# A written order for layer norm and SwiGLU forward, turned loads instead of TensorE turns, and stores on GpSimd's queue

## The chip, the cores and the metric

The kernel runs on one core of one Trainium2 chip. The metric is the time of one execution on the device in microseconds (us), as the median of several executions. A core has five engines with instruction streams of their own: TensorE (PE, with its weight loads PEld), VectorE (DVE), ScalarE (ACT), GpSimd (POOL) and SyncE (SP). A transfer (DMA) is issued by one of them and stands in the queue of that engine; 16 DMA engines move the data. A "turned load" is one DMA that writes the transpose of its source: rows become columns on the way. Turning can also be done on TensorE, as a matmul with the identity, whose result then has to be copied out of PSUM.

## The reference

The block is `x + s * silu(SwiGLU(LN(x)))`, where s comes from attention with a recurrent memory (64 segments of 32 tokens, 8 memory rows, 32 heads of 128). The kernel returns the output and the gradients of x, the initial memory, four attention weights and three SwiGLU weights. S is 2048 tokens, D is 640, F is 1728; everything is bf16.

```python
def _layernorm(x, axis=-1, eps=1e-05):
    m = jnp.mean(x, axis=axis, keepdims=True)
    v = jnp.var(x, axis=axis, keepdims=True)
    return (x - m) / jnp.sqrt(v + eps)

def _B_ref(x, w1, w3, w2):                      # SwiGLU
    gate = jnp.einsum('bsd,df->bsf', x, w1)
    up = jnp.einsum('bsd,df->bsf', x, w3)
    h = _silu(gate) * up
    return jnp.einsum('bsf,fd->bsd', h, w2)

xn = _layernorm(x, axis=-1)
s = _A_ref(xn, A_mem0, A_Wq, A_Wk, A_Wv, A_Wo, A_seg_len)   # recurrent attention, not shown
g = _silu(_B_ref(xn, B_w1, B_w3, B_w2))
out = x + s * g
# reference(): jax.vjp of this, applied to grad_out; returns out and nine gradients
```

## The kernel before

The program goes through these stages, one after the other: layer norm; SwiGLU forward; projections of the first tokens for the attention ("b0"); the forward chain over the memory; its output; the backward chain; the attention's weight gradients; the gradient of Wo; the gradient of w2; the SwiGLU backward with the layer norm backward; the gradients of w1 and w3. The change touches the beginning and the end, and in the middle only the loads of turned activations.

Layer norm, per tile of 128 tokens (16 tiles), and then the SwiGLU forward, per block of 512 tokens. `XN` and `XNT` are the normed activations in DRAM, straight and turned; `SLT` and `DUT` are two factors that the backward needs; `HB` is the hidden activation:

```python
            xn = io.tile([P, D], BF16, name="xn_t", tag="xn_t")
            nc.vector.tensor_scalar(xn[:], xt[:], rs, nmr[:], op0=ALU.mult, op1=ALU.add)
            k.dma(k.XN[tt * P:(tt + 1) * P, :], xn[:])
            # 5 TensorE transposes into pt, a copy, and the store of XNT
...
        nc.gpsimd.dma_start(Wv[:], k.A_Wv.rearrange("(dc p) h e -> p dc (h e)", p=P))
        k.x_rows(k.HRO, k.XN, nc.gpsimd)
        for blk in range(NBLK):
            if blk == 1:
                nc.gpsimd.dma_start(Wk_[:], k.A_Wk.rearrange("(dc p) h e -> p dc (h e)", p=P))
            b0 = blk * BLK
            xnT = io.tile([P, DC, BLK], BF16, name="xnT_b", tag="xnT_b")
            nc.scalar.dma_start(xnT[:], k.XNT[:, b0:b0 + BLK].rearrange("(dc p) t -> p dc t", p=P))
            hBT = io.tile([P, FC, BLK], BF16, name="hBT", tag="hBT")
            for fc in range(FC):                       # 14 chunks of hidden columns, the last has 64
                # 5 matmuls into pg (gate), 5 into pu (up), 512 columns each
                nc.scalar.activation(sig[:fsz], pg[:fsz], ACT.Sigmoid)
                nc.vector.tensor_tensor(sl[:fsz], pg[:fsz], sig[:fsz], ALU.mult)
                nc.scalar.copy(ut[:fsz], pu[:fsz])
                nc.vector.tensor_tensor(hBT[:fsz, fc, :], sl[:fsz], ut[:fsz], ALU.mult)
                nc.vector.scalar_tensor_tensor(ds[:fsz], sig[:fsz], 1.0, sl[:fsz], op0=ALU.subtract, op1=ALU.mult)
                nc.vector.tensor_tensor(ds[:fsz], sig[:fsz], ds[:fsz], ALU.subtract)
                nc.vector.tensor_tensor(ds[:fsz], ds[:fsz], ut[:fsz], ALU.mult)
                nc.sync.dma_start(k.SLT[fc * P:fc * P + fsz, b0:b0 + BLK], sl[:fsz])
                nc.sync.dma_start(k.DUT[fc * P:fc * P + fsz, b0:b0 + BLK], ds[:fsz])
            for ti in range(BLK // P):                 # second half, per 128 tokens
                # 28 matmuls of 320 columns (hBT with w2s) into pz; gb, dz, gs on VectorE and their stores on SP
                # 5 TensorE transposes of gs (store of GST), 14 of hBT, copies, store of HB
```

The first attention projection begins with the turned activations:

```python
        xs = io.tile([P, DC, k.NB0], BF16, name="b0x")
        nc.sync.dma_start(xs[:], k.XNT[:, 0:k.NB0].rearrange("(dc p) t -> p dc t", p=P))
```

The end of the kernel: gradient of w2 (`w2a`), SwiGLU backward in blocks of 256 tokens (`pghb`, `pgxb`, the turns `ptt5`), gradients of w1 and w3 (`wa`):

```python
                    for tt in range(NT):
                        pt = psA.tile([P, DC, P], BF16, name="gzp", tag="gzp")
                        for dc in range(DC):
                            nc.tensor.transpose(pt[:, dc, :], gz[:, tt, dc * P:(dc + 1) * P], k.ident[:])
                        k.copy(gzT[:, :, tt * P:(tt + 1) * P], pt[:], eng='vs'[tt % 2])
                    # w2a: 28 accumulators, 16 matmuls of 320 columns each, from hb and gz; stores of out9 on SP
...
                    for b0 in range(0, S, BLK):        # 8 blocks
                        for f0 in range(0, FC, 2):
                            # loads of two chunks of SLT and DUT (sl5, du5) on ScalarE's queue
                            for c in range(2):
                                # 5 matmuls of 256 columns (w2T with gzT) into pg ("pghb", two buffers)
                                nc.vector.tensor_tensor(ggT[0:fsz, fc, :], pg[0:fsz, :], du[0:fsz, c, :], ALU.mult)
                                nc.vector.tensor_tensor(guT[0:fsz, fc, :], pg[0:fsz, :], sl[0:fsz, c, :], ALU.mult)
                        for ti in range(BLK // P):
                            # 56 matmuls of 320 columns into pgx ("pgxb", one buffer); every fourteenth has 64 rows
                            for i, (gT, dst) in enumerate(((ggT, ggtok[:, tt, :]), (guT, gut[:]))):
                                pt = psC.tile([P, 2 * 1024], BF16, name="ptt5", tag="ptt5", bufs=2)
                                for fc in range(FC):
                                    fsz = fszs[fc]
                                    nc.tensor.transpose(pt[:, fc * P:fc * P + fsz], gT[0:fsz, fc, tcol], k.ident[0:fsz, 0:fsz])
                                nc.vector.tensor_copy(dst[:, 0:704], pt[:, 0:704])
                                nc.scalar.copy(dst[:, 704:F], pt[:, 704:F])
                            nc.sync.dma_start(GU[rows, :], gut[:])
                            # layer norm backward: gxn and six more operations; out1 stored on SP
...
                gutok = up.tile([P, NT, F], BF16, name="gutok_all")
                # 8 loads of GU; then 320 matmuls of 432 columns on ggtok, 320 on gutok ("wa")
```

Of the kernel before, what the change touches and what calls it, by code (L numbers as in the profile page):

```python
# [9 lines left out]
BF16 = mybir.dt.bfloat16  # L10
# [30 lines left out]
class K:  # L41
# [55 lines left out]
    def setup_consts(self):  # L97
# [9 lines left out]
        self.mean_all = const.tile([P, self.NT], F32, name="mean_all")  # L107
# [44 lines left out]
    def setup_dram(self):  # L152
# [7 lines left out]
        self.XNT = mk("XNT", (D, S))  # L160
        self.SLT = mk("SLT", (F, S))
        self.DUT = mk("DUT", (F, S))
        self.HB = mk("HB", (S, F))
# [3 lines left out]
        self.GST = mk("GST", (D, S))  # L167
# [200 lines left out]
def phase3_Afwd(k, W4, Wv, Wk_):  # L368
# [5 lines left out]
    with tc.tile_pool(name="b0", bufs=1) as io, tc.tile_pool(name="b0s", bufs=3) as stp, \  # L374
            tc.tile_pool(name="b0p", bufs=4, space=bass.MemoryType.PSUM) as ps:
        xs = io.tile([P, DC, k.NB0], BF16, name="b0x")
        nc.sync.dma_start(xs[:], k.XNT[:, 0:k.NB0].rearrange("(dc p) t -> p dc t", p=P))
# [21 lines left out]
    with tc.tile_pool(name="ast", bufs=1) as st, tc.tile_pool(name="achain", bufs=1) as ch, \  # L399
# [22 lines left out]
        def ride_ld(t):  # L422
            x0 = k.NB0 + 24 * t
            b, sub = t // 4, t % 4
            if sub == 0 and x0 < S:
                w = min(96, S - x0)
                rt = ch.tile([P, DC, 96], BF16, name="ride", tag="ride")
                nc.sync.dma_start(rt[:, :, 0:w], k.XNT[:, x0:x0 + w].rearrange("(dc p) s -> p dc s", p=P))
                rides[b] = (rt, w)
# [339 lines left out]
def gx_ld(k, xs, x0, eng):  # L769
    w = min(P, k.S - x0)  # L770
    eng.dma_start(xs[:, :, 0:w], k.GST[:, x0:x0 + w].rearrange("(dc p) t -> p dc t", p=P))
# [13 lines left out]
def phase3b_out(k, Wo, W0, W4):  # L785
# [12 lines left out]
    with tc.tile_pool(name="oio", bufs=1) as io, tc.tile_pool(name="oac", bufs=1, space=bass.MemoryType.PSUM) as pa, \  # L798
# [60 lines left out]
        def gox_ld(x0):  # L859
            xs = io.tile([P, DC, P], BF16, name="g0x", tag="g0x", bufs=2)  # L860
            gx_ld(k, xs, x0, nc.scalar)
            st["gx", x0] = xs
# [61 lines left out]
def phase4_Abwd(k, out2, WoT, WvT, WkT, WqT, later):  # L924
# [3 lines left out]
    with tc.tile_pool(name="gst", bufs=1) as st, tc.tile_pool(name="gchain", bufs=1) as ch, \  # L928
# [25 lines left out]
        def ride_ld(t):  # L954
# [3 lines left out]
            if sub == 3:  # L958
                rt = ch.tile([P, DC, 96], BF16, name="gride", tag="gride")
                nc.sync.dma_start(rt[:], k.GST[:, 96 * b:96 * b + 96].rearrange("(dc p) s -> p dc s", p=P))  # L960
# [278 lines left out]
        def gox(x0, cg, b):  # L1239
            if cg == 0 and b == 0:  # L1240
                uu["gx"] = ch.tile([P, DC, P], BF16, name="gx0", tag="xp", bufs=1)
                gx_ld(k, uu["gx"], x0, nc.gpsimd)
# [252 lines left out]
def phase6b_gWo(k, gow, orr0, out6, gz, late):  # L1495
# [4 lines left out]
    with tc.tile_pool(name="o6", bufs=1) as hp, tc.tile_pool(name="o6i", bufs=2) as io, \  # L1500
# [21 lines left out]
        def rows_ld(q):  # L1522
            orrs[q] = io.tile([P, NW, 512], BF16, name="orr", tag="orr")
            for a in range(2):
                rows = slice(h * P * a, h * P * (a + 1))
                nc.sync.dma_start(orrs[q][:, h * a:h * a + h, :],
                                  k.OR[rows, 512 * q:512 * q + 512].rearrange("(t p) c -> p t c", p=P))
        rows_ld(1)
        for qd in range(8):
            orr = orrs[qd]  # L1530
            for jp in range(2):
# [4 lines left out]
                if qd > 1 and late:  # L1536
                    out_, in_ = late.pop(0)
                    if in_ is k.w2:
                        turned_load(k, out_, in_)
                    else:  # L1540
                        nc.scalar.dma_start(out_, in_)
# [8 lines left out]
                for j in range(2):  # L1550
# [4 lines left out]
                    nc.sync.dma_start(out6f[hh * P:(hh + 1) * P, :], ot[:])  # L1555
# [5 lines left out]
def phase1_ln(k: K):  # L1561
    nc, tc = k.nc, k.tc
    D, DC, NT = k.D, k.DC, k.NT
    with tc.tile_pool(name="ln_io", bufs=3) as io, tc.tile_pool(name="ln_sm", bufs=4) as sm, \
            tc.tile_pool(name="ln_ps", bufs=2, space=bass.MemoryType.PSUM) as ps:
        half = D // 2
        assert half <= nc.vector.BN_STATS_FMAX
        for tt in range(NT):
            xt = io.tile([P, D], BF16, name="xt", tag="xt")
            k.dma(xt[:], k.A_x[tt * P:(tt + 1) * P, :])  # L1570
            stats = sm.tile([P, 2, nc.vector.BN_STATS_DIM], F32, name="stats", tag="stats")
            xv = xt[:].rearrange("p (a b) -> p a b", a=2)
            nc.vector.bn_stats(stats[:, 0, :], xv[:, 0, :])
            nc.vector.bn_stats(stats[:, 1, :], xv[:, 1, :])
            mv = sm.tile([P, nc.vector.BN_AGGR_DIM], F32, name="mv", tag="mv")
            nc.vector.bn_aggr(mv[:], stats[:])
            rs = k.rstd_all[:, tt:tt + 1]
            nc.scalar.activation(rs, mv[:, 1:2], ACT.Sqrt, bias=k.eps_t[:], scale=1.0)
            nc.vector.reciprocal(rs, rs)
            nc.vector.tensor_copy(k.mean_all[:, tt:tt + 1], mv[:, 0:1])  # L1580
            nmr = sm.tile([P, 1], F32, name="nmr", tag="nmr")
            nc.vector.tensor_tensor(nmr[:], mv[:, 0:1], rs, ALU.mult)
            nc.vector.tensor_scalar(nmr[:], nmr[:], -1.0, None, op0=ALU.mult)
            xn = io.tile([P, D], BF16, name="xn_t", tag="xn_t")
            nc.vector.tensor_scalar(xn[:], xt[:], rs, nmr[:], op0=ALU.mult, op1=ALU.add)
            k.dma(k.XN[tt * P:(tt + 1) * P, :], xn[:])
            pt = ps.tile([P, DC, P], BF16, name="lnT", tag="lnT")
            for dc in range(DC):
                nc.tensor.transpose(pt[:, dc, :], xn[:, dc * P:(dc + 1) * P], k.ident[:])
            xnT = io.tile([P, DC, P], BF16, name="xnT_t", tag="xnT_t")  # L1590
            k.copy(xnT[:], pt[:])
            k.dma(k.XNT[:, tt * P:(tt + 1) * P].rearrange("(dc p) t -> p dc t", p=P), xnT[:])

def phase2_Bfwd(k: K, Wv, Wk_):
    nc, tc = k.nc, k.tc
    D, DC, S, F, FC = k.D, k.DC, k.S, k.F, k.FC
    BLK = 512
    NBLK = S // BLK  # L1600
    fszs = [min(P, F - fc * P) for fc in range(FC)]
    with tc.tile_pool(name="bw", bufs=1) as wp, tc.tile_pool(name="bio", bufs=2) as io, \
            tc.tile_pool(name="bwork", bufs=2) as wk, \
            tc.tile_pool(name="bps", bufs=2, space=bass.MemoryType.PSUM) as ps, \
            tc.tile_pool(name="bps1", bufs=1, space=bass.MemoryType.PSUM) as ps1:
        w1s = wp.tile([P, DC, F], BF16, name="w1s")
        k.dma(w1s[:], k.w1.rearrange("(dc p) f -> p dc f", p=P))
        w3s = wp.tile([P, DC, F], BF16, name="w3s")
        k.dma(w3s[:], k.w3.rearrange("(dc p) f -> p dc f", p=P))
        w2s = wp.tile([P, FC, D], BF16, name="w2s")  # L1610
        for fc in range(FC):
            k.dma(w2s[:fszs[fc], fc, :], k.w2[fc * P:fc * P + fszs[fc], :])
# [296 lines left out]
```

## Time and profile before

| what | value |
|---|---|
| median of 3 runs | 5573.68 us (5566.38 to 5581.09) |
| profiled run, first to last instruction | 5562.0 us |
| mean granted TensorE clock | 0.952 of full speed |
| busy: TensorE, VectorE, ScalarE, GpSimd | 4935.7, 2343.2, 1783.4, 1570.4 us |
| moved by DMA | 808.27 MB, mean 145 GB/s |
| stage from 0 to 62 us (layer norm): busy TensorE, VectorE | 11.12, 33.26 us |
| 328 to 4915 us (attention, forward and backward): busy TensorE | 4095.12 us of 4587 |

The profile is one execution. A line that groups instructions names the source line, the engine, and the tiles written and read. The view of waits names the engine and operation that stood, what it stood on, the total, how often, and the longest. The view of transfers gives the queue, the count, the KB of one and the time from issue to landing. The view by stretches gives busy time, with the number of instructions, for each engine. The number after the engine's share in a stage tells whether it can be the bound there; which wait ended last tells what the bound is.

### The profile page before, as it was taken

Reading aid. Unit: us, or ns where it says so; the run is one execution under the profiler, and the core shown is the slowest. Engines: PE = TensorE matmul, PEld = TensorE weight load, DVE = VectorE, ACT = ScalarE, POOL = GpSimd, SP = SyncE. Lnnn points to the kernel's source line nnn. Section 1 sums busy time; section 2 is a strip of 40 time slices with the busy share of each in tenths; the row PEclk is TensorE's granted clock in tenths of the full one; section 3 lists DMA queues with packets and bytes.
Section 4 is the critical chain, followed back from the end, with each engine's and each line's share of the span. In section 5 each row is a group of like instructions: output and inputs, shape, how many; then the busy total and the mean of one; then the engine's idle time right before and its main releaser. Section 6 shows DMA issues by size and latency. Waiting matters only on the chain. (4 is left out here: it accounts for less than half of the span.)

```text
span 5562.0 us, 164947 instructions
## 1 busy us (share of the span) xinstructions
PE 4935.7 (89%) x66673; PEld 3152.5 (57%) x67020; DVE 2343.2 (42%) x7398; ACT 1783.4 (32%) x4953; POOL 1570.4 (28%) x2604
## 2 busy tenths in 40 slices
PE   4987888888888677989999997999999999998999
PEld 2554555555555444656666665566556655666665
DVE  5833555555555323444444542233223322311451
ACT  2422555555555322323333332233113312300111
POOL 0000344444444212333333333243224322310000
PEclk9998999999999778999999998999999999999999
DMA  7553455555555686666666666354335433657332
GB/s 252 171 185 90 137 152 153 158 156 162 153 151 143 152 171 155 176 186 184 186 184 178 185 169 130 76 124 99 94 74 126 98 87 83 162 166 188 106 117 92
DMA packets 1126617, 808.27 MB, mean 145 GB/s; under 512 B 672971, under 2 KB 1016679, under 8 KB 1123179
## 3 DMA queue, kind: packets, MB, share of 16 engines
q1 hardware_dynamic: 884995, 555.06, 37.3%
q0 software_dynamic: 91472, 144.46, 9.3%
q10 hardware_dynamic: 149388, 98.17, 6.3%
q8 instruction: 529, 8.67, 0.7%
q14 instruction: 233, 1.91, 0.1%
HBM read 468.47 MB, written 296.78 MB: 138 GB/s over the span
## 5 line engine op out<-in xcount | busy, mean ns | idle before, releaser
L1403 PE MATMUL wg<-gr,hr 120*128 120x512 bf16 (+1 forms) x2640 | 592.9, 386 | 17.3 <-DVE dST L1335 13.1
L1381 PE MATMUL g<-w,gT 128*128 128x320 bf16 x3840 | 548.4, 299 | 0.0
L1403 PEld LDWEIGHTS <-hr 120*128 120x128 bf16 (+1 forms) x2640 | 258.9, 99 | 343.1 <-issue 52.1
L1381 PEld LDWEIGHTS <-gT 128*128 128x128 bf16 x3840 | 368.8, 98 | 136.3
L243 POOL DMA_DIRECT2D r<-GOS x256 | 143.4, 564 | 795.8 <-PE r6p L1345 704.8
L90 DVE CAST wgo<-wg 128x512 bf16<-128x512 f32 x72 | 47.5, 688 | 589.2 <-issue 281.8
L316 PEld LDWEIGHTS <-hx 128*32 128x32 bf16 x7680 | 179.7, 97 | 169.4 <-issue 12.4
L90 DVE CAST stg<-bank 128x512 bf16<-128x512 f32 x256 | 177.0, 692 | 208.4 <-PE bank L316 199.4
L335 PEld LDWEIGHTS <-gkv 128*8 128x8 bf16 x8192 | 189.7, 87 | 107.4 <-DVE gkv L1012 23.8
L619 ACT ACTIVATE xP<-xsp,xnm 120x120 bf16<-120x120 f32 (+1 forms) x704 | 240.5, 376 | 8.5 <-DVE xnm L615 4.5
L1390 DVE TENSOR_TENSOR ghacc<-ghacc,g 128x320 f32<-128x320 f32 x240 | 117.0, 487 | 277.7 <-PE g L1381 277.7
L92 ACT CAST wgo<-wg 128x512 bf16<-128x512 f32 x48 | 25.8, 589 | 640.3 <-PE wg L1403 640.3
L1163 POOL DMA_DIRECT2D DSR<-gdS x176 | 101.6, 577 | 426.5 <-DVE gdS L1161 383.3
L1348 ACT CAST gr<-r6p 120x512 bf16<-120x512 f32 (+1 forms) x176 | 103.3, 587 | 361.7 <-PE r6p L1345 340.8
L668 POOL DMA_DIRECT2D OR<-xv x163 | 94.6, 580 | 418.9 <-ACT xv L667 287.0
L92 ACT COPY gT<-t6g 128x960 bf16<-128x960 bf16 (+5 forms) x216 | 167.0, 792 | 119.9 <-PE t6g L1364 117.0
L630 POOL TENSOR_TENSOR xP<-xP,xrz 120x480 bf16<-120x480 bf16 x163 | 161.8, 992 | 141.0 <-ACT xP L619 96.5
L1161 DVE SCALAR_TENSOR_TENSOR gdS<-gdp,Dx,gPr 120x120 bf16<-120x120 f32 (+1 forms) x680 | 182.7, 330 | 0.0
L1232 PE MATMUL gbank<-WqT,ident 128*128 128x512 bf16 x453 | 159.5, 402 | 20.1 <-issue 12.2
L335 PE MATMUL bank<-Wo,oTm 128*32 128x320 bf16 x4032 | 177.0, 329 | 0.1
L316 PE MATMUL gbank<-WoT,gox 128*32 128x512 bf16 x2560 | 153.6, 387 | 24.6 <-POOL gox L967 21.2
L1364 PE MATMUL t6g<-ident,gr 120*128 120x120 bf16 (+1 forms) x2112 | 172.0, 221 | 3.3 <-DVE wgo L90 2.7
(339 smaller groups left out, 10991.0 us busy)
## 6 DMA issues: line engine op xcount, KB each, us to landing
QVS<-stg SPq DMA_DIRECT2D x128, 256.0 KB
gqv<-QVS SPq DMA_DIRECT2D x108, 192.0 KB
vTt<-VTD SPq DMA_DIRECT2D x64, 320.0 KB
VTD<-gvT POOLq DMA_DIRECT2D x168, 120.0 KB, 3.6
OR<-xv POOLq DMA_DIRECT2D x163, 120.0 KB, 2.5
DSR<-gdS POOLq DMA_DIRECT2D x168, 112.5 KB, 3.4
dS<-DSR SPq DMA_DIRECT2D x168, 112.5 KB
P<-PR SPq DMA_DIRECT2D x168, 112.5 KB
```

What stands on the lines that cost most here:

```text
L90: return nc.vector.tensor_copy(out, in_)
L92: return nc.scalar.copy(out, in_)
L243: eng.dma_start(d, src if src.shape[0] > 1 else src[0])
L316: k.nc.tensor.matmul(bank[32 * g:32 * g + 32, :], x[:, dc, :], W[:, dc, c0:c0 + 512], start=(dc == 0), stop=(dc == k.DC - 1), tile_positio ...
L335: k.nc.tensor.matmul(pm[p0:p0 + nq, 0:320], x[:, h, :], W[:, h, 320 * b:320 * b + 320], start=(first and i == 0), stop=(last and i == 15), ...
L619: nc.scalar.activation(Pb[0:n, j, 0:n], sp[0:n, j, :], ACT.Exp, bias=nmx[0:n, j:j + 1], scale=k.scale, accum_out=Z[0:n, j:j + 1])
L630: eng.tensor_tensor(Pb[0:n, :, 0:n], Pb[0:n, :, 0:n], bc_last(rz[0:n], n), ALU.mult)
L1161: nc.vector.scalar_tensor_tensor(dS[0:n, j, :], dp[0:n, j, :], Dx[0:n, j:j + 1], Pr[0:n, j, :], op0=ALU.subtract, op1=ALU.mult)
L1232: nc.tensor.matmul((bA if g in ("W1", "G1", "G2") else bB)[:], k.ident[:], WqT[:, 0, 0:512], start=True, stop=True)
L1364: nc.tensor.transpose(pt[:, i - i0, j, :], st["g", u, i][0:n, j * P:(j + 1) * P], k.ident[0:n, 0:n])
L1381: nc.tensor.matmul(pg[:], ring[:, i, j, r0:r0 + P], Ws[qd][i][:, j, 320 * h:320 * h + 320], start=(i == 0 and j == 0), stop=(i == 2 and j ...
L1403: nc.tensor.matmul(accs[dc][:], hr[0:n, tl, dc * P:(dc + 1) * P], st["g", NTL * qd + tl, i][0:n, :], start=(tl == 0), stop=(tl == NTL - 1))
```

## The change

It is meant to free TensorE and the copy engines of the turns, to run the layer norm beside the first SwiGLU block instead of ahead of it, and to keep SP's queue for the turned loads:

- Layer norm and SwiGLU forward become one stage whose instructions keep, on each engine, the order in which they are written (`in_order`). Four tiles of layer norm come first, the other twelve are spread over block 0. The second half of a block (`up`) is spread over the first chunks of the next.
- The turned copies `XNT` and `GST` in DRAM are gone; whoever needs them makes a turned load from `XN` or `GS`. All turned loads are on SP's queue.
- `HB` and `GU` are stored turned and loaded back through turned loads. The turns of gz and ggT go from SBUF to SBUF.
- Stores of the forward stage, of out6, out9, out1, out7 and out8 move to GpSimd's queue. The loads of Wv and Wk and the copies of HRO stay on it.
- Last chunks of 64 rows are padded with zeros to 128 rows; in the SwiGLU backward pg gets four buffers and pgx two.

The core of the diff; cuts are marked with "...":

```diff
@@ b0
-        nc.sync.dma_start(xs[:], k.XNT[:, 0:k.NB0].rearrange("(dc p) t -> p dc t", p=P))
+        for x0 in range(0, k.NB0, 112):
+            turned_load(k, xs[:, :, x0:x0 + 112], k.XN[x0:x0 + 112, :])
... (the rides of the attention chains likewise)
@@ def gx_ld (backward chain and weight gradients)
-    eng.dma_start(xs[:, :, 0:w], k.GST[:, x0:x0 + w].rearrange("(dc p) t -> p dc t", p=P))
+    turned_load(k, xs[:, :, 0:w], k.GS[x0:x0 + w, :])
@@ def phase6b_gWo: rows_ld and out6 from nc.sync to nc.gpsimd; the loads of hb:
-        for t0 in range(0, NT, 2):
-            rows = slice(t0 * P, (t0 + 2) * P)
-            late.append((hb[:, t0:t0 + 2, :], k.HB[rows, :].rearrange("(t p) f -> p t f", p=P)))
+        for f in range(0, F, 432):
+            late.append((hb[:, :, f:f + 432], k.HB[f:f + 432, :]))
@@ def phase12_ln_Bfwd (new)
+        def fetch(blk):
+            xnT = io.tile([P, DC, BLK], BF16, name="xnT_b", tag="xnT_b")
+            for i in range(2):
+                turned_load(k, xnT[:, :, i * BLK // 2:(i + 1) * BLK // 2], k.XN[blk * BLK + i * BLK // 2:blk * BLK + (i + 1) * BLK // 2, :])
...
+        def hidden(blk, fc):
...            (matmuls, sig and ut as before)
+            sl = wk.tile([P, BLK], BF16, name="sl", tag="sl", bufs=3)
+            nc.vector.tensor_tensor(sl[:fsz], pg[:fsz], sig[:fsz], ALU.mult)
+            nc.vector.tensor_tensor(hBT[:fsz, fc, :], sl[:fsz], ut[:fsz], ALU.mult)
+            ds = wk.tile([P, BLK], BF16, name="ds", tag="ds", bufs=3)
+            nc.vector.scalar_tensor_tensor(ds[:fsz], sig[:fsz], 1.0, sl[:fsz], op0=ALU.subtract, op1=ALU.mult)
+            nc.vector.tensor_tensor(ds[:fsz], sig[:fsz], ds[:fsz], ALU.subtract)
+            nc.vector.tensor_tensor(ds[:fsz], ds[:fsz], ut[:fsz], ALU.mult)
+            nc.gpsimd.dma_start(k.SLT[fc * P:fc * P + fsz, cols], sl[:fsz])
+            nc.gpsimd.dma_start(k.DUT[fc * P:fc * P + fsz, cols], ds[:fsz])
...
+        for tt in range(TB):
+            ln_ld(tt)
...            (w1s, w3s: first 512 columns of each, then the rest, on ScalarE's queue)
+        for tt in range(TB):
+            ln_stats(tt)
+        ln_rstd(0, TB)
+        for tt in range(TB):
+            ln_rows(tt)
+        fetch(0)
...
         for blk in range(NBLK):
             for fc in range(FC):
+                hidden(blk, fc)
+                if blk == 0:
...                    (statistics of 12 tiles at fc 0 to 5, their rows at fc 6 to 11)
+                    if fc == 9:
+                        fetch(1)
+                    if fc == 12:
+                        nc.gpsimd.dma_start(Wv[:], k.A_Wv.rearrange("(dc p) h e -> p dc (h e)", p=P))
+                    if fc == 13:
+                        k.x_rows(k.HRO, k.XN, nc.gpsimd)
+                elif fc == 0:
+                    hidden_out(blk - 1)
...
+                elif fc < 9 and fc % 2 == 0:
+                    up(blk - 1, fc // 2 - 1)
...
+                elif fc == 9 and blk + 1 < NBLK:
+                    fetch(blk + 1)
+                elif fc == 11 and blk == 1:
+                    nc.gpsimd.dma_start(Wk_[:], k.A_Wk.rearrange("(dc p) h e -> p dc (h e)", p=P))
...
+        hidden_out(NBLK - 1)
+        in_order(k, start)
@@ def phase5_Bbwd_ln
-                        pt = psA.tile([P, DC, P], BF16, name="gzp", tag="gzp")
-                        for dc in range(DC):
-                            nc.tensor.transpose(pt[:, dc, :], gz[:, tt, dc * P:(dc + 1) * P], k.ident[:])
-                        k.copy(gzT[:, :, tt * P:(tt + 1) * P], pt[:], eng='vs'[tt % 2])
+                        turned_load(k, gzT[:, :, tt * P:(tt + 1) * P], gz[:, tt, :])
...
-                        tc.tile_pool(name="c5pc", bufs=2, space=bass.MemoryType.PSUM) as psC, \
-                        tc.tile_pool(name="c5pd", bufs=1, space=bass.MemoryType.PSUM) as psD:
+                        tc.tile_pool(name="c5pc", bufs=4, space=bass.MemoryType.PSUM) as psC, \
+                        tc.tile_pool(name="c5pd", bufs=2, space=bass.MemoryType.PSUM) as psD:
...
-                            for (t_, src) in ((sl, k.SLT), (du, k.DUT)):
+                            for (t_, src, q) in ((sl, k.SLT, nc.scalar), (du, k.DUT, nc.gpsimd)):
...            (both loads on q)
+                                turned_load(k, ggtok[:, b0 // P:b0 // P + 2, fc * P:fc * P + fsz], ggT[0:fsz, fc, :])
+                        nc.gpsimd.dma_start(GU[0:FR, cols].rearrange("(c p) t -> p c t", p=P), guT[:, 0:FC - 1, :])
...            (the turns ptt5 and their copies are removed)
-                    nc.scalar.dma_start(gutok[:, t0:t0 + 2, :], GU[t0 * P:(t0 + 2) * P, :].rearrange("(t p) f -> p t f", p=P))
+                for f in range(4):
+                    turned_load(k, gutok[:, :, 432 * f:432 * f + 432], GU[432 * f:432 * f + 432, :])
```

Each DMA signals through a semaphore. In the built program the DMAs of SP and ScalarE share eight of them and those of GpSimd another eight, taken in turn, and a DMA is issued only when the one that used its semaphore before has landed.

## Prediction

> **What bounds the kernel now.** I split the span at its stages first, with the view that gives the busy time of each engine by stretch. TensorE is busy 89% of the whole span, but not evenly. The stretches that the change rewrites are these (columns: stretch and length, busy time and instruction count of TensorE, weight loads, VectorE, ScalarE, GpSimd; then granted clock, DMA share, GB/s):
>
> ```profile
> 62.00:328.00 266.00, 222.67 (x1293) 116.61 (x1311) 176.43 (x360) 99.73 (x161) 3.13 (x4) 0.93 0.56 190
> 5092.00:5180.00 88.00, 73.60 (x528) 47.13 (x524) 10.57 (x24) 9.87 (x20) 1.49 (x3) 0.92 0.46 94
> 5180.00:5439.00 259.00, 238.67 (x1904) 163.58 (x1905) 145.05 (x352) 42.77 (x64) 26.59 (x23) 0.99 0.38 117
> 5439.00:5562.00 123.00, 118.43 (x640) 62.97 (x639) 12.00 (x22) 9.68 (x21) 1.39 (x1) 0.99 0.25 99
> ```
>
> The SwiGLU forward (62 to 328) and the layer norm before it (0 to 62) end where the first attention projection starts, at 328.1. Inside it, the waits are:
>
> ```profile
> ACT sig L1634 <- DVE ds L1643: 55.3, 26, 11.4
> DVE gb L1660 <- ACT sz L1658: 39.6, 15, 8.2
> PE pg L1628 <- DVE sl L1636: 21.2, 3, 9.5
> DVE sl L1636 <- DMA SLT<-sl: 12.7, 3, 11.1
> DVE ds L1642 <- DMA DUT<-ds: 17.1, 6, 4.4
> ```
>
> VectorE sets the pace there, and VectorE itself waits for its own stores to land. The cause is a burst on GpSimd's queue, shown by the transfers of 0 to 330 (last column: us from issue to landing) and by the times of issue:
>
> ```profile
> Wv<-in_A_Wv_dram POOLq DMA_DIRECT2D x1, 5120.0 KB, 28.1
> Wk<-in_A_Wk_dram POOLq DMA_DIRECT2D x1, 5120.0 KB, 41.5
> HRO<-XN POOLq DMA_DIRECT2D x1, 2520.0 KB, 17.3
> HRO<-XN POOLq DMA_DIRECT2D x1, 40.0 KB, 27.4
> ```
> ```profile
> 63.24 0.81 POOL L251 DMA_DIRECT2D HRO<-XN  x1 [59.24 <-DMA XNT<-xnT_t]
> 66.23 0.90 POOL L1614 DMA_DIRECT2D Wv<-in_A_Wv_dram  x1 [2.19 <-DVE sl L1636]
> 67.13 0.54 POOL L253 DMA_DIRECT2D HRO<-XN  x1
> 67.66 0.89 POOL L1618 DMA_DIRECT2D Wk<-in_A_Wk_dram  x1
> ```
>
> Added up, they land at 80.5, 94.3, 94.5 and 109.2: in order of issue, 13.8 us for Wv once it is at the head, 14.7 us for Wk. A copy of 40 KB took 27.4 us because it stood behind Wv. This carries my main doubt below.
>
> At the end of the kernel I read the chain that ended last from 4900 on (start, length, what):
>
> ```profile
> 5101.56 18.03 DMA x<-in_B_w_dram
> 5182.63 9.75 DMA sl<-SLT
> 5247.27 0.83 DVE gxn L1790
> 5254.88 3.37 DMA sl<-SLT
> 5278.71 0.83 DVE gxn L1790
> ```
>
> The w2 gradient (5092 to 5180) loses its time at a single place, a turned weight load that holds the queues and thereby the copies of the turned gz. The SwiGLU backward runs in blocks of 31.4 us (5278.71 - 5247.27) with about 3.4 us of waiting for SLT in each.
>
> **What the Trainium skill says.** "DMA: Bandwidth & Descriptors", Queues, rings and completion order: each DMA engine takes turns between the queue rows it has work for, by packets. So a store on SP's queue gets its turn beside Wv, and one on GpSimd's queue stands behind it. The landings above agree with the second half. "Advanced Engine Details and Errata", X-Bar Transpose (TRN2): turned transfers are about as fast as plain ones, 350 to 400 GB/s. This trace has less: w1T, 1664 x 640 bf16 or 2.13 MB, kept SP for 8.06 us (264 GB/s), and 655 KB of w6 take a median of 2.5 us (262 GB/s). I use 260. "VectorE: DVE Perf Modes", The DRAIN you can't avoid: the next operation does not start until the pipe is empty. The trace differs: independent operations of 0.42 us start 0.34 us apart, and only dependent ones wait (0.45 us from ds L1643 at 120.40 to ds L1644 at 120.85). That matters, since a written order puts dependent ones next to each other. "TensorE: Matmul & The Clock Gate", Part 1: The HAM clock gate, says that idle gaps bring half rate; after the stall above, the clock from 5116 to 5130 is 0.56, which agrees.
>
> **The change, part by part.**
>
> Costs of one: a matmul of 512 columns 0.215 us (240 of b0pb in 51.6 us), of 320 columns 0.137 us (1280 of oa in 175.6 us), of 256 columns 0.108 us (half of the first, an estimate). Where every fourteenth matmul has 64 rows, 14 of pgxb took 2.11 us, so 0.151 each; the change pads it with zeros to 128, which I take to give 0.137.
>
> (1) Start. Today x queues behind the weights (first statistics at 19.4 us) and the first hidden matmul starts at 61.9. After: x goes first (4 tiles by about 5 us), four tiles of statistics at about 1.05 us, rows, store. The second half of the turned load reuses the semaphore of the last w3 load, so it waits until 5.7 MB are in: at the 311 GB/s of the first 24 us about 19 us. Then 1.3 us of turning and 2 us to land: first matmul at 22.5, VectorE's first sl near 26.
>
> (2) VectorE per hidden chunk, in written order: sl 0.70 (hBT depends on it), hBT 0.34, ds 0.70 (the next depends on it), ds 0.45, ds 0.34 = 2.53 us. TensorE's 10 matmuls need 2.15. So VectorE bounds: 56 x 2.53 = 141.7. Second half, per 128 rows: gb 0.86, dz 0.86, gs 0.42, dz 0.42, about 2.55 x 16 = 40.8, against 28 x 0.137 = 3.84 on TensorE. Twelve late layer norm tiles at 1.05 + 0.36 = 16.9. Sum 199.4, so 26 + 199.4 = 225. The blocks mix 14 chunks and 4 second halves, where the two engines have nearly the same work (45.6 against 45.5 us), so I add 3 us of mismatch for each of three blocks and 6 for the last second halves: 240.
>
> (3) What the move to GpSimd's queue costs. Wv is issued after chunk 12 of block 0, HRO after chunk 13, both ahead of the next stores. sl and ds have three buffers, so chunk n waits for the store of chunk n - 3. Wv 14 us and then HRO 13 to 17 us, less three chunks at 2.5 us and one second half: about 24 us of stall. Wk in block 1: 14.7 - 7.6 + 2 = 9 us. The forward then ends near 273. The region of b0x is released only when the last HB store (1.8 MB, behind everything) has landed, and b0x is itself a turned load: +10. First attention projection at 283 instead of 328.1: 45 us gained.
>
> (4) Middle (328 to 5092). The same matmuls in the same order. The turned loads of the rides are small. One loss: the first gx load now stands on SP behind a turned WqT load (4.92 us at 2031.7) and TensorE waits for it at once: 7 us lost.
>
> (5) w2 gradient: 448 matmuls x 0.137 = 61.4, plus some 5 us of accumulator changes, nothing of gz on TensorE or on the copies. w1T, w3T and 16 turned tiles of gz need 6.9 MB at 260 GB/s = 27 us on SP and lie beside it. 88 becomes 66: 22 gained.
>
> (6) SwiGLU backward, per block of 256: 70 x 0.108 + 112 x 0.137 = 22.9 us of TensorE against 31.4 today; 56 turns at 0.069 (28 in 1.93 us) are gone. With four accumulators VectorE still bounds the first part of each block: 13 chunks x 0.68 plus 2.6 of layer norm and 0.8 of gxn = 12.5 us, in which TensorE has 9 to do. So 26 to 27 us per block, and 9 us for the first one as today: 259 becomes 219, 40 gained. The 14 turned ggT tiles per block keep SP perhaps 1 us each, an estimate from the shortest turned load seen, 1.21 us for 164 KB.
>
> (7) Last stage: GU is turned in four loads, 7.1 MB / 260 GB/s = 27 us, ready some 40 us after the stage begins; the 320 matmuls on ggtok take 59 us. Hidden.
>
> Sum: 45 - 7 + 22 + 40 = 100 us; 5573.7 - 100 = 5474. A little of TensorE's clock comes back where the stall of 5108 to 5122 goes, and I take 5470.
>
> **Rivals.** (a) The stores on GpSimd's queue cost nearly nothing, because the stall that I charge is a burst that the old kernel also had (VectorE waited 30 us for SLT and DUT). Then b0 starts near 255 and the time is about 5440. For: bandwidth is the same. Against: the 40 KB copy. (b) Crossbar on the path: the eight hardware DMA semaphores are shared between the sl loads and the turned ggT tiles, and each DMA waits for the one eight before it. If a turned tile lands late, sl is late, and each block keeps its 31 us: 5510. For: today's 3.4 us on SLT per block. (c) Turned loads slower than I think in all places (on-chip to on-chip turns occur nowhere in this trace): gz not ready at the end of the w2 gradient, GU not ready at 59 us: 5530.
>
> **Range and chances.** (a) and (b) move the sum by -30 and +40, the start by 10 either way. 5415 to 5520 should hold it 8 times in 10. The 2% line is at 5462, close to my value: faster 0.46, same 0.52, slower 0.02.
>
> **What would show it.** First b0pb near 283 (255 under a). Long waits of sl and ds on SLT and DUT after Wv, HRO and Wk. VectorE at 2.5 us per chunk. No gap after 5092 - 45; gxn to gxn 26 to 27 us (31 under b); TensorE without a wait on gutok_all. I am wrong if block 1 shows no stall, if TensorE waits for ggtok or gz, or if the attention stages differ by over 15 us.

## The result, and the profile after

The changed kernel takes 5542.33 us (median of 4 runs, 5529.12 to 5547.01) against 5570.03 us for the kernel before in the same comparison: ratio 0.9944, 95% interval 0.992 to 0.9968. I had predicted 5470 with a range of 5415 to 5520. The direction was right and the size wrong: some 28 us instead of 100.

The stages of the changed kernel, by the view of busy time by stretches (columns as in the prediction):

```profile
27.00:278.50 251.50, 201.05 (x1008) 101.59 (x1007) 192.68 (x389) 78.62 (x132) 98.94 (x179) 0.93 0.53 192
278.50:301.50 23.00, 0.00 (x0) 0.00 (x0) 2.54 (x4) 0.62 (x1) 3.76 (x6) 0.60 0.91 228
...
4925.00:5123.00 198.00, 177.12 (x1281) 126.09 (x1282) 30.85 (x66) 12.82 (x32) 55.66 (x93) 0.95 0.92 208
5123.00:5193.00 70.00, 66.69 (x448) 42.04 (x448) 6.58 (x16) 4.53 (x12) 17.41 (x34) 0.98 0.75 154
5193.00:5419.00 226.00, 197.79 (x1457) 142.98 (x1457) 124.77 (x316) 12.44 (x30) 96.84 (x133) 0.96 0.77 167
5419.00:5541.00 122.00, 116.95 (x640) 62.52 (x639) 13.70 (x25) 10.23 (x22) 7.35 (x12) 0.99 0.43 98
```

Four things are to be seen. The gradient of w2 and the SwiGLU backward (5123 to 5419) shrank from 347 to 296 us, as meant. The last stage is unchanged. Between the forward's last matmul (278.5) and the first attention projection (301.5) TensorE does nothing for 23 us while the DMA engines are 91% busy. And the gradient of Wo (4925 to 5123), which I had not touched in the prediction, takes 198 us where it had 177; TensorE does the same 177 us of work in it.

The waits of the forward (engine and operation, what it stood on, total, times, longest):

```profile
DVE sl L1621 <- DMA SLT<-sl: 33.6, 4, 11.4
...
PE pg L1614 <- DMA xnT_b<-XN: 27.1, 1, 27.1
...
PE b0pb L391 <- DMA b0x<-XN: 23.2, 1, 23.2
...
DVE gb L1649 <- ACT sz L1647: 5.2, 4, 1.5
```

and its transfers between 0 and 330 us (last column: us from issue to landing, median):

```profile
SLT<-sl POOLq DMA_DIRECT2D x52, 128.0 KB, 2.2
...
HB<-hBT POOLq DMA_DIRECT2D x4, 1664.0 KB, 15.0
Wv<-in_A_Wv_dram POOLq DMA_DIRECT2D x1, 5120.0 KB, 17.0
Wk<-in_A_Wk_dram POOLq DMA_DIRECT2D x1, 5120.0 KB, 18.0
...
HRO<-XN POOLq DMA_DIRECT2D x1, 2520.0 KB, 28.8
```

A store of SLT lands 2.2 us after its issue (median). The four waits of VectorE fall behind Wv, HRO and a store of HB (22.2 us) and behind Wk (11.4 us), together the 33.6 us that I had charged as 24 + 9. GpSimd's own instructions show that not only the queue holds the stores (start, length, in brackets its idle time and what ended it):

```profile
100.16 0.59 POOL L1663 DMA_DIRECT2D HB<-hBT  x1 [10.85 <-DMA SLT<-sl]
...
114.96 0.54 POOL L1627 DMA_DIRECT2D SLT<-sl  x1 [13.10 <-DMA HRO<-XN]
```

The store of SLT at 114.96 could not be issued earlier: GpSimd stood 13.10 us until HRO had landed, whose semaphore this store takes next.

At the end, the chain that ended last has new links in it (start, length, what):

```profile
4927.26 43.23 PE oa L1543 x317
...
4972.19 17.38 DMA out_dram<-wgoo
...
4989.64 10.66 DMA out_dram<-wgoo
...
5002.60 29.76 DMA orr<-OR
5032.40 89.56 PE oa L1543 x638
```

and TensorE's wait in it:

```profile
PE oa L1543 <- DMA orr<-OR: 17.9, 2, 17.7
```

A load of orr took 29.76 us from issue to landing, and the stores of out6 before it 17 and 11 us; TensorE then stood for 17.7 us. In the kernel before no transfer stands in this part of the chain.

(In the table of the profile before, the busy time of TensorE from 328 to 4915 is 4095.29 us, not 4095.12.)

### The profile page after: what moved, and what is told of

Its sections match the earlier page's. It is cut to its first block, busy times and chain, and to the rows that moved or that the text cites. A ratio compares the mean times of both kernels' runs of the same rounds, so it can differ in the third digit from the quotient of the medians.

```text
span 5541.6 us, 163422 instructions
## 1 busy us (share of the span) xinstructions
PE 4916.3 (89%) x66108; PEld 3104.6 (56%) x66108; DVE 2314.4 (42%) x7275; ACT 1719.4 (31%) x4861; POOL 1788.8 (32%) x2982
## 3 DMA queue, kind: packets, MB, share of 16 engines
q0 software_dynamic: 115504, 222.88, 13.6%
## 5 line engine op out<-in xcount | busy, mean ns | idle before, releaser
L1401 PE MATMUL wg<-gr,hr 120*128 120x512 bf16 (+1 forms) x2640 | 592.9, 386 | 17.4 <-DVE dST L1333 13.1
L90 DVE CAST wgo<-wg 128x512 bf16<-128x512 f32 x72 | 47.5, 688 | 588.3 <-PE wg L1401 292.0
L1230 PE MATMUL gbank<-WqT,ident 128*128 128x512 bf16 x640 | 204.3, 403 | 0.0
L1131 POOL DMA_DIRECT2D VTD<-gvT x176 | 130.5, 745 | 148.6 <-ACT gvT L1130 117.3
L332 PE MATMUL bank<-Wo,oTm 128*32 128x320 bf16 x4032 | 175.0, 327 | 0.6 <-DVE oTm L535 0.3
```

The lines of the kernel that those rows point to most:

```text
L90: return nc.vector.tensor_copy(out, in_)
L332: k.nc.tensor.matmul(pm[p0:p0 + nq, 0:320], x[:, h, :], W[:, h, 320 * b:320 * b + 320], start=(first and i == 0), stop=(last and i == 15), ...
L1230: nc.tensor.matmul((bA if g in ("W1", "G1", "G2") else bB)[:], k.ident[:], WqT[:, 0, 0:512], start=True, stop=True)
L1401: nc.tensor.matmul(accs[dc][:], hr[0:n, tl, dc * P:(dc + 1) * P], st["g", NTL * qd + tl, i][0:n, :], start=(tl == 0), stop=(tl == NTL - 1))
```

## The experiments

I read stages by TensorE's first instruction in each: the time from the first hidden matmul to the end of the last second half ("forward"); the start of b0; the two memory chains; the gradient of Wo; the gradient of w2; the SwiGLU backward. Runs with edits in different stages are read stage by stage.

**The same two kernels again.** No edit.

> The changed kernel once more, unaltered. The two memory chains lasted 1407.6 + 1397.9 = 2805.5 us in its first profile against 2774.8 in the kernel before, with some 38 us more at half clock, and I had predicted no change there. Theory C (the clock dips in the chains come by chance): this profile differs from 2805.5 by more than 6 us, and the dips lie at other steps. Rival R (the turned rides disturb the chains in every execution): within 4 us of 2805.5. The other stages should repeat within 1 us.

Time 5509.55 us. The chains took 1397.6 + 1393.5 = 2791.1 us instead of 2805.5. What I had not expected: the gradient of Wo took 176.4 us instead of 195.7, with nothing changed. So this stage is at an edge, and one profile of it decides little. The other stages repeated: b0 starts at 301.1 (301.6), the gradient of w2 68.9 (70.5), the SwiGLU backward 228.8 (225.6).

> The kernel before, unaltered, for its spread. Theory C (the middle differs by chance): its two chains together lie somewhere between 2770 and 2805 us, like those of the changed kernel (2805.5, 2791.1, 2793.3, 2798.5). Rival R (turned rides cost time, most of it in the backward chain, where the run with plain rides had 1385.6 us and those with turned rides 1393.5 to 1400.0): forward chain about 1393, backward chain 1386 or less, sum at most 2780. Gradient of Wo: 176.7 us again, since nothing there was at the edge.

> The kernel before a third time. If the changed kernel's forward chain is really longer (1393 to 1410 us in nine profiles with the changed middle, mean 1400, against 1392.8 and 1390.1), this one has at most 1394; if the difference is chance, 1396 or more is as likely.

The kernel before had chains of 1390.1 + 1398.6 = 2788.7 us and then 1403.4 + 1396.6 = 2800.0, after 2774.8 in the first profile; its gradient of Wo 176.7 and 175.0. So the rival (the change lengthens the chains in every execution) lost its footing: 2774.8 is the lowest of the three sums. Thirteen profiles of the changed kernel and its variants have 2787.0 to 2816.8, mean 2797.4; three of the kernel before have a mean of 2787.8. A difference of 10 us is neither shown nor excluded. In the trace's clock records the chains with more half-clock time tend to be the longer ones (242 us of it in the 2774.8, 281 in the 2805.5).

**Rides.** Edit: `turned_load(rt, XN[...])` becomes a plain load of the same shape, values not those of the reference.

> The small loads that ride along in the two chains are plain loads of the same shape again (they read the same bytes without turning them, so the values in the attention are others). Rival R (turned rides slow the chains): the chains together return to some 2775 us. Theory C (chance): they stay anywhere between 2770 and 2815, and the time at half clock follows the sum; nothing else moves.

1401.4 + 1385.6 = 2787.0 us: inside the scatter above. The turned rides are not seen to cost anything. Its gradient of Wo took 189.3 us.

**Large transfers on SP's queue.**

```diff
-nc.gpsimd.dma_start(Wv[:], ...)
+nc.sync.dma_start(Wv[:], ...)          # the copies of HRO and the load of Wk likewise
```

> The loads of Wv and Wk and the copies of HRO are issued on SP's queue, behind the turned loads of the next block; nothing else changes. Theory Q (the stores of the forward stage stand behind these large transfers in GpSimd's queue): VectorE's long waits for SLT (33.6 us) all but vanish, and the time from the first hidden matmul to the last second half falls from 251.2 us to about 220. Rival a (it is bandwidth, whichever queue): it stays above 242.

Forward 239.5 us, between both expectations. The waits for SLT fell from 33.6 to 15.8 us, one of 10.5: the store of HB, 1,664 KB on GpSimd's queue, now met the copies of HRO and took 23.4 us to land. GpSimd stood 13.6 us for its semaphore, and the small stores waited behind that. The move takes one large transfer out of the way of the stores, not the meeting.

**Large transfers elsewhere, cut up, or out.** Three more edits on the same question:

```diff
 s2: Wv, Wk -> nc.sync; HRO -> nc.scalar, written in the b0 loop; HB -> nc.scalar
 s3: Wv, Wk in 5 loads, HRO in 4, HB in 2 stores, all on nc.gpsimd, one per chunk or two
 w_end: Wv, Wk and HRO issued after hidden_out(NBLK - 1)
```

> Three edits. (1) Forward: Wv and Wk on SP's queue, the copies of HRO later, beside the attention projections, and the stores of HB on ScalarE's queue; SLT, DUT and the others stay alone on GpSimd's. Theory Q: no store stands behind a large transfer any more, and the time from the first hidden matmul to the last second half is 222 us or less (251.2 in the changed kernel, 239.5 with only the move to SP). Rival a (bandwidth): 235 or more. (2) The gradient of Wo paced as in the run beside it: 176 to 178 us. (3) The first turned load of gs ahead of the turned load of WqT: the gap from the last turns of the output stage to its first matmul falls from 23 to about 18 us.

The forward got longer, 272.6 us. The copies of HRO, written for the b0 stage, have no data to wait for and were put at 93.5 us by the scheduler; ScalarE's queue then held 4.2 MB, and this is what followed (issues and operations of ScalarE in order of time: start, length):

```profile
95.53 42.64 ACTq L1665 DMA_DIRECT2D HB<-hBT  x1
138.21 1.09 ACTq L1635 DMA_DIRECT2D Gt<-in_grad_out_dram  x2
139.43 0.60 ACT L1619 ACTIVATE sig<-pg 128x512 bf16<-128x512 f32 x1 [43.84 <-DMA HB<-hBT]
```

The issue of a 64 KB store held ScalarE for 42.6 us, and with it every sigmoid. Whether the length of the queue or a shared semaphore held it was not separated. This run says nothing on theory Q. Its edit (3), the turned gs ahead of WqT, worked as expected: from the last turns of the output stage to that first matmul it took 18.6 us instead of 24.2.

> Two edits. (1) Forward: everything stays on GpSimd's queue, with as many bytes, but cut up and spread: Wv and Wk in five loads each, one per chunk or two, the copies of HRO in four pieces in the third block, HB in two stores. Theory Q (a store stalls because it stands behind 14 to 31 us of transfers, more than the three buffers of sl and ds cover): each piece takes some 3 us, three chunks cover 7.5, and the time from the first hidden matmul to the last second half falls from 251 to 225 or less. Rival a (the bytes themselves cost the time): it stays at 240 or more. (2) The turned load of w2T is issued after those of w1T and w3T, beside the gradient of w2, instead of during the gradient of Wo. Theory T (a turned load and the loads of orr slow each other): the time in which they meet falls from some 120 to 85 us, and the gradient of Wo lies at 176 to 184 us; the gradient of w2 stays within 3 us of 70, since SP has some 50 us of turned loads in it.

Forward 250.9 us, as without the edit. The long stalls of block 0 were gone (none over 2.4 us), but VectorE still waited 29.9 us for SLT in all: the pieces of Wk, 1 MB for each chunk of some 2.5 us, with the turned loads of the next block and a store of HB beside them, produced a wait of 13.3 us of their own. The second edit of this run did not take place: the scheduler moved the load of w2T back into the gradient of Wo (187.9 us there). So up to here the cost of the transfers was open, and the last edit measured it by itself:

> Two edits in two stages. (1) Wv, Wk and the copies of HRO leave the forward: they are issued at its end, so the attention projections begin later; only the time from the first hidden matmul to the last second half counts here. My step (3) put 24 + 9 = 33 us on these transfers: that time falls from 251.2 to 216 to 224 us. If the pace of the engines and not the transfers sets it (rival a: cutting them up changed nothing), it stays above 240. (2) The plain loads of hb once more, for a second sample of the gradient of Wo without turned loads of hb: theory T says 176 to 179 us; 185 or more would say that the 178.3 us of the first sample were chance.

```profile
27.00:246.00 219.00, 192.14 (x1008) 99.82 (x1007) 192.47 (x389) 78.73 (x132) 95.84 (x175) 0.98 0.48 161
```

The forward takes 218.8 us without them, 32.4 less than 251.2: my step (3) had 33. So the size of the cost is shown. That it comes from the order in GpSimd's queue is shown only in part: with Wv, Wk and HRO on another queue the forward gained 11.7 us, with all in pieces nothing. How much of the rest is the semaphores taken in turn, the bandwidth or the turned loads beside them was not separated. In this run the cost moved to the next stage:

```profile
PE b0pb L391 <- DMA b0x<-XN: 39.5, 1, 39.5
```

The turned loads of b0x now stood beside Wv and Wk; b0 started at 285.3 but took 21 us longer.

**The start of b0.** In the changed kernel the last store of HB and the six turned loads of b0x stand one after the other (views of GpSimd and of SP in order of time):

```profile
282.72 1.18 POOL L1662 DMA_DIRECT2D HB<-hBT  x1
```
```profile
16.51 4.78 SPq L277 DMA_TRANSPOSE xnT_b<-XN  x2
...
290.67 12.45 SPq L277 DMA_TRANSPOSE b0x<-XN  x6
```

HB lands at 290.2, 7.5 us after issue, and only then are the six turned loads issued, over 12.45 us. Edit of s1: `hidden_out(NBLK - 1)` ahead of the last second halves.

> Three edits in three stages. (1) The last store of HB is issued ahead of the last four second halves. If the first attention projection waits for that store, as the release of its region says, b0 starts at about 294 instead of 301; if the turned loads of b0x themselves are the limit, it stays at 299 or later. (2) Gradient of Wo: the five turned loads are held in place, one per 22 us, each behind a store of out6 on SP that waits for its copies. Theory P (they hurt because nothing holds them on SP's queue, so all are issued at the start of the stage): 176 to 178 us, where the changed kernel had 195.7, 176.4 and, with edits elsewhere only, 189.3 and 199.5. If their sum is too much for the stage in any order, it stays spread over 180 to 200. (3) The du loads of the SwiGLU backward are on ScalarE's queue again: if they are late because they stand behind the stores of GU, that stage falls from 226 to about 219; if not, it stays within 2 us.

(1) b0 starts at 297.5 us: 4 gained, not 7, and here is why. The turned loads of b0x now begin at 277.8 and meet the last stores (transfers between 279.5 and 302; last column as above):

```profile
GB<-gb POOLq DMA_DIRECT2D x2, 160.0 KB, 19.6
DZ<-dz POOLq DMA_DIRECT2D x2, 160.0 KB, 19.0
GS<-gs POOLq DMA_DIRECT2D x2, 160.0 KB, 20.0
b0x<-XN SPq DMA_TRANSPOSE x5
```

Stores of 160 KB that otherwise land in 2 us take 19 to 20, and the fourth turned load held SP for 13.8 us. Side by side, the turned loads, these stores and the loads of Wq on ScalarE's queue all took longer; this run doesn't say which of them stretched which.

(3) The loads of du on ScalarE's queue: SwiGLU backward 229.3 us, no gain. (2) is told next.

**The gradient of Wo.** Edits, each in its own run:

```diff
 hb_plain: -turned_load(k, out_, in_)   +nc.sync.dma_start(out_, in_)   # hb, as many bytes, not turned
 s1, s2:   one turned load at tt = 2, 4, 6, 8, 10, each behind a store of out6 on SP; wgoo with 4 buffers
 orr_act:  -nc.gpsimd.dma_start(orrs[q]...)   +nc.scalar.dma_start(orrs[q]...)
```

> The four turned loads of hb during the gradient of Wo become plain loads of as many bytes on the same queue and at the same places (the gradient of w2 is then formed from unturned values). Theory T (turned loads take so much of the DMA engines that the loads of orr land late): the gradient of Wo falls from 195.7 us to 182 or less. Rival S (orr stands in GpSimd's queue behind the stores of out6): it stays at 190 or more.

178.3 us, and 180.6 in the second sample, just above the 176 to 179 that I expected (the run w_end_hb_plain, whose gradient of w2 is likewise formed from unturned values); TensorE waited 1.7 and 2.4 us for orr. In the first sample:

```profile
PE oa L1546 <- DMA orr<-OR: 1.7, 1, 1.7
```

The stage with turned loads of hb and no edit in it had 195.7, 176.4, 189.3 (rides_plain), 199.5 (w_sp), 177.7 (psc2), 187.9 (s3) and 207.9 (best1, below): five of seven are above both samples, two below. The pacing of s1 and s2 made it 251.2 and 225.3 us, the opposite of theory P. In s1 the one wait is:

```profile
PE oa L1543 <- DMA orr<-OR: 63.0, 5, 21.0
```

Put at regular distances, every turned load of hb meets a load of orr. In s1 it then holds SP for 31 to 43 us, where the changed kernel has 12 to 31, and a load of orr takes a median of 27.1 us instead of 11.1. One behind the other from the start of the stage, as in the changed kernel, is the milder form, probably since one load of orr is there in advance. These two runs also put some stores of out6 behind the turned loads on SP, which may have delayed the loads of orr as well.

> The loads of orr during the gradient of Wo are issued on ScalarE's queue; the stores of out6 and the loads of the epilogue stay on GpSimd's. Rival S (orr lands late because it stands in GpSimd's queue behind other transfers): TensorE never waits for orr and the stage is 176 to 178 us. Theory T (turned loads and orr slow each other, whatever the queue): with turned loads of hb in flight an orr piece still needs 20 us or more from issue to being there, and the stage takes 185 us or more.

203.0 us, TensorE waits for orr:

```profile
PE oa L1543 <- DMA orr<-OR: 21.6, 4, 10.8
```

So taking orr out of GpSimd's queue is not enough. This doesn't clear the stores of out6, for ScalarE also copies for them: before it issued the load of orr at 5006.2 it stood 24.4 and 10.1 us until such a store had landed. What the turned loads do is seen in the packets. The same stage of the kernel before (4930 to 5106, second profile), of the changed kernel (4927 to 5122), of its second execution (4910 to 5087) and of hb_plain (4914 to 5092), in that order, and for the last three SP's queue (packets, MB, time of its packets as a share of 16 engines):

```profile
DMA packets 36051, 40.95 MB, mean 233 GB/s; under 512 B 10320, under 2 KB 32464, under 8 KB 36039
```
```profile
DMA packets 45329, 40.94 MB, mean 210 GB/s; under 512 B 37968, under 2 KB 38352, under 8 KB 45317
q1 hardware_dynamic: 36880, 9.68, 42.5%
```
```profile
DMA packets 45338, 40.99 MB, mean 232 GB/s; under 512 B 37968, under 2 KB 38352, under 8 KB 45326
q1 hardware_dynamic: 36880, 9.68, 33.2%
```
```profile
DMA packets 19665, 40.94 MB, mean 230 GB/s; under 512 B 10256, under 2 KB 10640, under 8 KB 19653
q1 hardware_dynamic: 11216, 9.68, 25.5%
```

The bytes are the same 41 MB. The turned loads of hb bring 27,700 packets under 512 B (37,968 - 10,256; 7.08 MB / 27,712 = 255 bytes each), and the same 9.68 MB of SP's queue keep the DMA engines busy for longer. Their share is 0.74 in the kernel before, 0.77 in hb_plain, 0.93 and 0.89 in the two executions of the changed kernel. But the execution with 176.4 us has as many packets as the one with 195.7: they put the stage at the edge, and what tips one execution over it stays open. So the turned loads of hb are the likely cause: without them the stage had 178.3 and 180.6 us, with them placed against orr 225 and 251. Two samples against a stage that two times in seven is as fast by itself are thin. That it is the number of packets, and not another property of turned loads, is argued from this view and was not tried apart.

**Accumulators or turns.** Edit: pools c5pc and c5pd with 2 and 1 buffers again.

> The accumulators of the SwiGLU backward are two and one again, instead of four and two; the turns stay off TensorE. If the gain there comes from the turns, as my step (6) has it, the stage stays within 4 us of 226; if the buffers carry it, it goes to 240 or more. All other stages as in the changed kernel.

Between both: 238.4 us.

```profile
5155.90:5394.30 238.40, 203.44 (x1457) 138.67 (x1457) 125.74 (x315) 12.44 (x30) 96.14 (x133) 0.99 0.70 159
```

Of the 34 us that this stage gained, the accumulators bring 11 (238.4, one profile, to 227.2, the mean of two), and the rest of the change in this stage 23 (261.0, the mean of three profiles, to 238.4): the turns taken off TensorE, with the padding and the other queues, which were not tried apart.

**A version with what was learned.** Both: forward pieces, early HB store, first turned gs ahead of WqT, and the turned xn stored once from the forward's own tile, so that b0x and the rides of the forward chain are plain loads (the store on SP's queue, `xnT_b` to `XNT`, after the third chunk of each block). best1 also writes w2T late, with no effect, as in s3. best2 instead gives orr a third buffer, the region of its first part.

> The two edits of the run beside it, and: the last store of HB ahead of the last second halves; the first turned load of gs ahead of WqT; the turned xn of each block, which the forward has in SBUF anyway, is stored to DRAM once, and b0x and the rides of the forward chain are plain loads of it. If the wait for b0x (23 us) is mostly that of six turned loads and the store of HB, b0 starts at 257 us or before, against 301; if it is the release of the region by the last stores, at 265 or later. With the middle as in the other runs (2788 to 2805 us for the chains) I expect 5465 to 5490 us in all. Without an effect of the pieces it would be 5500 or more.

5526.69 us (5 runs, 5499.27 to 5543.25), ratio 0.991 (0.9879 to 0.9941). The forward took 242.2 us, and b0 starts at 283.8, not 257 or 265. With a plain load of b0x and the store of HB out of its way, TensorE still stands:

```profile
PE b0pb L391 <- DMA b0x<-XNT: 15.1, 1, 15.1
```

Three loads of Wq are issued at the same moment and stores are still landing; in these 15.1 us 328 GB/s move. So of the 23.2 us, 15 remain without turning. The gradient of Wo took 207.9 us in the profile and spoiled the rest.

> Forward as in best1 (Wv, Wk, HRO and HB in pieces, the last HB store early, turned xn stored once for b0x and the rides), the first turned gs ahead of WqT, and a third buffer for orr in the gradient of Wo, taken from the region that its first part leaves free: each load of orr is then issued 22 us earlier, and 43 us cover it instead of 22. If orr's late landing (up to 30 us) is all that varies in that stage, it is 176 to 179 us in every execution, and the median falls from the 5526.7 us of best1 to about 5505, with a smaller spread. If more turned loads only stretch further, it stays above 185.

5511.55 us (4 runs, 5504.9 to 5528.77), ratio 0.9906 (0.988 to 0.9931). The forward took 250.3 us, b0 starts at 292.0. TensorE no longer waits for orr; the stage takes 185.8, not 176 to 179, because the stores of out6 now hold the copies (6.2 us). Its median is the lowest of the versions that were timed in several runs, but its interval overlaps that of the changed kernel, and one execution of that took 5509.55: it beats the kernel before; that it beats the changed one is not shown.

## Why the prediction was wrong, point by point

By profiles, the changed kernel's mean is 5524.5 us (two) and that of the kernel before 5576.5 (three): 52 us gained, where the medians of the comparison say 28. The scatter of the chains and of the gradient of Wo, up to 30 us between executions, lies between these two numbers. Of the 100 us of the prediction this leaves 48 missing, or 72 by the medians; the table divides the 48. The steps that failed are the "+10" for b0x in (3), which was 23, and "the same matmuls in the same order" in (4), which left out the gradient of Wo:

| step | predicted | profiles after | missing us |
|---|---|---|---|
| (1) first hidden matmul | 22.5 | 27.1, 27.0 | in the next |
| (1)-(3) start of b0 | 283, 45 gained | 301.6, 301.1, 28 gained against a mean of 329.7 | 17 |
| (4) b0 to the gradient of Wo | 7 lost | 18 lost (4599.6 to 4617.7, means) | 11, in the scatter |
| none: gradient of Wo | unchanged | 195.7, 176.4, against 176.1 | 10 |
| (5) gradient of w2 | 66, 22 gained | 70.5, 68.9, 18 gained | 4 |
| (6) SwiGLU backward | 219, 40 gained | 225.6, 228.8, 34 gained | 6 |
| (7) last stage | hidden | 122.6, 122.6 | 0 |

**Step (1)** was short by 4.6 us. The second turned half was issued at 19.0, as worked out, but its matmuls began at 27.1: 8 us instead of 3.3, with the weights in flight beside it.

**Steps (2) and (3)**: the size of the forward holds. Its last matmul ended at 278.3 where I had 273, of which 4.6 came from the start, and without the transfers it took 218.8 us where (2) has 240 - 22.5 = 217.5. Taking them out gave 32.4 us for my 33. Rival (a), nearly free stores, is refuted by that. But 33 was partly luck: 14 + 13 to 17, less three chunks at 2.5 and a second half of 2.55, is 17 to 21 and not 24, and I had left out the store of HB and the semaphores that hold GpSimd. The term that failed is the "+10" for b0x: it measured 23 us. I had seen that b0x waits for the last store of HB and is turned; I sized the turning with a rate taken from loads without company. The six loads, 0.86 MB, took 12.45 us to issue beside Wq: 69 GB/s, not 260. Nor is it the turning alone: with HB out of the way the wait was 19.8 us turned (s1: 277.7 to 297.5) and 15.1 and 14.7 plain (best1, best2). What I left out is above all what moves beside the load.

**Step (4)**, "the same matmuls in the same order", looked only at TensorE. It held for the turned gs: the stage from the output to that load got 7 to 8 us longer (134.0 to 141.3, means), and with the order changed it had 137.3. For the gradient of Wo it is the missing step. I had counted the loads of hb there as moved to another queue and turned, and never asked what else moves during it. It is the one stage in which orr must come just in time, 2,560 KB every 22 us, and with the turned loads beside it, it went over the edge in some executions.

**Steps (5) and (6)** had the right mechanism: no wait for gz or gutok, no turned tile late. The blocks of the backward are 26.0 to 30.5 us apart (mean 27.7 by gxn), against 26 to 27; the wait that remains is TensorE's for ggT:

```profile
PE pgxb L1807 <- DVE ggT L1794: 20.7, 17, 4.1
```

Rival (b), blocks of 31 us, was wrong. Rival (c), slow on-chip turns, was wrong too: a turned ggT tile held SP for a median of 1.20 us, near my estimate of 1. I had credited the turns with nearly all of it, while a third came from the accumulators.

**The Trainium skill's statements.** "DMA: Bandwidth & Descriptors", Queues, rings and completion order, that each DMA engine takes turns between the queues by packets, may bear on it: SP's 9.68 MB took 42.5 and 33.2% of the DMA engines' time in that stage in 36,880 packets, and 25.5% in 11,216. Whether the packets that the profile counts are those of the page, no run here shows. I had used it for the order within a queue and not for what the change adds. "Advanced Engine Details and Errata", X-Bar Transpose (TRN2), expects 350 to 400 GB/s of turned loads; here gutok, 7.08 MB with little beside it, held SP for 32.6 us (217 GB/s), and one load of hb beside orr, 1.77 MB, for 31.3 us (56 GB/s).

## What to carry to other kernels

When a plain load becomes a turned one, size it with what else moves at that moment: list the loads that must come just in time in the same stage, and count its packets beside its bytes. A transfer moved to a queue that nothing holds up goes out as soon as its buffer is free: the first load of hb 5.1 us after the stage's first matmul, in the kernel before 45.8. Look up when that is. And a stage that waits for nothing by a small margin needs several executions before one reads it.

## What the runs showed of the hardware that I had not expected

- The turned loads of hb went in packets of about 255 bytes. With turned loads under way, transfers on GpSimd's queue landed late in s1: stores of 160 KB in 19 to 20 us instead of 2 (Wq was loading too), loads of orr in a median of 27.1 us, against 11.1 in the changed kernel and 9.6 in hb_plain.
- One unaltered kernel took 195.7 and 176.4 us for the same stage in two executions, and 5509.55 to 5547.01 us in all.
- Issuing a 64 KB store held ScalarE for 42.6 us behind 4.2 MB in its queue (s2; what held it was not separated). A turned load held SP for 7 us (hb in orr_act) to 58 us (w2T in hb_plain) in the gradient of Wo.
- A store on GpSimd's queue was not even issued for 13.1 us, until HRO, issued earlier, had landed.
